# Softmax of a group in its own iteration, between pieces of the product with V; the last V in quarters

## Chip, cores and metric

The kernel runs on one core of a Trainium2 chip. The metric is the device time of one execution in microseconds; the median of three runs counts. The engines are TensorE (PE, its weight loads PEld), VectorE (DVE), ScalarE (ACT), GpSimd (POOL) and SyncE (SP), which here only issues transfers.

## What is computed

One decode step of a transformer block: layer norm, attention of one new token over a cache of 4,096 keys and values, then a second layer norm and a small MLP. Four batches, 32 heads, head size 128, all in bf16.

```python
B, Sq, D = 4, 1, 640;  H, Sk, Dh = 32, 4096, 128;  F = 1728
q = (layernorm(x) @ wq).reshape(B, Sq, H, Dh).transpose(0, 2, 1, 3)
scores = einsum("bhqd,bhkd->bhqk", q, k_cache) * Dh ** -0.5
o = einsum("bhqk,bhkd->bhqd", softmax(scores), v_cache)
h = x + o.transpose(0, 2, 1, 3).reshape(B, Sq, H * Dh) @ wo
y = layernorm(h) @ w1 + b1
h2 = h + (y * tanh(softplus(y))) @ w2
```

K and V are 134 MB each, and each element is used once. Everything else is small: wq and wo have 5.2 MB each, w1 and w2 together 4.4 MB.

## The kernel before

The 128 pairs of batch and head are taken in 32 groups of four heads of one batch: group g has head block `hq = g // 4` and batch `b = g % 4`. A group's K is one tile `kt` of 4.19 MB, its V one tile `vt` of the same size; 32 partitions belong to each head, and each partition holds 128 keys. There are two buffers for K and two for V.

**Scores.** `mul_and_sum` (L328) handles half of the keys (a part), in two steps: VectorE multiplies 64 of the 128 columns of `kt` by the query in place (L337), then TensorE adds the products up by eight matmuls with the identity (L344) into `s`, which has two buffers. After the second step `finish_sum` (L353) has VectorE add the last eight columns into `s_sb` (L356). So a group has four multiplies, four passes of eight matmuls, and two sums.

**Softmax.** `softmax` (L363) is a generator with two steps. First: VectorE takes the maximum of each partition (`pm`, L367) and TensorE transposes it (`tr`, L369). Second: VectorE takes the maximum of each head (`mx`, L374), TensorE spreads it over the partitions (L382), ScalarE copies it (`nbs`, L384) and makes four exponentials into `e2` (L387), which has two buffers.

**Product with V.** `pv_moving` (L241) makes 32 matmuls (L245) into `p`, which ScalarE copies to `p_sb` (L253, one buffer). `add_blocks` (L255) adds its four diagonal blocks into `ot` by small matmuls (L259). Groups 30 and 31 use `pv` (L267) after the loop instead: 128 small matmuls with V as the stationary operand (L271).

**The loop** (L397). The order of each engine's instructions is the order in which the program writes them. In iteration g, part 0 makes the scores of g, and between its two steps comes the second sum of g - 1 and the first step of its softmax; after the second step of part 0 comes the second step of that softmax. In part 1, between its two steps, come the first sum of g, `add_blocks(g - 2)`, and when b is 1 also `row_sums` (L283, L291) and `normalise` (L294) of the head block before. After part 1 SP issues the load of K for g + 2, which waits until the scores have read the buffer; then comes the product for g - 1; sometimes `project` (L318); then SP issues V of g + 1, which waits until the product has read its buffer. For the first seven iterations the queries of the next head block follow (L191, L205). The last K and the last V are loaded in two halves each (L93).

**After the loop** SP issues w1 (L463) and w2 (L464 to L467); w1 and most of w2 share one K buffer. Then come the second sum and the softmax of group 31, `pv(30)`, `row_sums`, `pv(31)`, `normalise`, `project`, the layer norm and the MLP. The first matrix product of the MLP (L514) writes `h1_ps`, part of which VectorE clears first (L509).

Of the kernel before, what the change touches and what calls it, by code (L numbers as in the profile page):

```python
# [8 lines left out]
FP32 = mybir.dt.float32  # L9
# [7 lines left out]
def kernel(  # L17
# [23 lines left out]
    nc = tc.nc  # L41

    B, Sq, D = A_x.shape
    _, H, Sk, Dh = A_k_cache.shape
    F = B_w1.shape[1]
    N = B * Sq
# [3 lines left out]
    R = Sk // PH  # L50
    NP = 2
# [3 lines left out]
    NG = HQ * N  # L55
# [14 lines left out]
    FREM = F - C2 * 128  # L70
    FC = C2 + 1
# [6 lines left out]
    kpool = ctx.enter_context(tc.tile_pool(name="kpool", bufs=KBUFS))  # L78
    vpool = ctx.enter_context(tc.tile_pool(name="vpool", bufs=VBUFS))
# [5 lines left out]
    out_rows = out.rearrange("b s (c p) -> (b s c) p", p=128)  # L85


    def load_kv(pool, tag, cache, g):
        hq, b = divmod(g, N)
        t = pool.tile([128, R, Dh], BF16, tag=tag, name=f"{tag}{g}")  # L90
        view = cache[b, G * hq : G * (hq + 1)].rearrange("h (p r) d -> (h p) r d", p=PH)

        np_ = NP if g == NG - 1 else 1  # L93
        for i in range(np_):
            r0, r1 = i * R // np_, (i + 1) * R // np_
            nc.sync.dma_start(out=t[:, r0:r1, :], in_=view[:, r0:r1, :])
        return t

    def load_k(g):
        return load_kv(kpool, "kt", A_k_cache, g)  # L100

    def load_v(g):
        return load_kv(vpool, "vt", A_v_cache, g)

    x_bf = consts.tile([N, D], BF16)
    nc.scalar.dma_start(out=x_bf[:, :], in_=x_rows[:, :])
# [63 lines left out]
    ps = ps_cm.__enter__()  # L170
# [58 lines left out]

    J = 4  # L230
    NSTAT = 2

    def ot_of(g):
        hq, b = divmod(g, N)
        if b == 0:
            ot[hq] = ps.tile([128, N, G], FP32, tag="ot", name=f"ot{hq}")
        return ot[hq][:, b, :]

    blocks = {}

    def pv_moving(g):  # L241
        vt = vts.pop(g)
        p_ps = ps.tile([J * G, J * Dh], FP32, tag="p", name=f"p{g}")
        for r in range(0, R, J):
            nc.tensor.matmul(  # L245
                p_ps[:, :],
                lhsT=e2[g % NE2][:, r : r + J, :].rearrange("p j q -> p (j q)"),
                rhs=vt[:, r : r + J, :].rearrange("p j d -> p (j d)"),
                start=(r == 0),
                stop=(r == R - J),  # L250
            )
        blocks[g] = work.tile([J * G, J * Dh], FP32, tag="p_sb", bufs=1, name=f"p_sb{g}")
        nc.scalar.copy(out=blocks[g][:, :], in_=p_ps[:, :])  # L253

    def add_blocks(g):  # L255
        o = ot_of(g)
# [10 lines left out]
    def pv(g):  # L267
        vt = vts.pop(g)
        o = ot_of(g)
        for r in range(R):  # L270
            nc.tensor.matmul(  # L271
                o,
                lhsT=vt[:, r, :],
                rhs=e2[g % NE2][:, r, :],
                start=(r == 0),
                stop=(r == R - 1),
            )
# [15 lines left out]
    def normalise(hq):  # L293
        nc.vector.tensor_tensor(  # L294
            out=otn[:, hq, :, :],
            in0=ot.pop(hq)[:, :, :],
            in1=rls.pop(hq)[:, :, :],
            op=ALU.mult,
        )
# [28 lines left out]
    def mul_and_sum(g, part):  # L328

        hq, b = divmod(g, N)  # L330
        r0 = part * RP
        kt = kts[g][:, r0 : r0 + RP, :]
        s_ps = ps.tile([128, RP, W], FP32, tag="s", bufs=2, name=f"s{g}_{part}")
        s_of[g, part] = s_ps
        for k in range(NQ):
            d0 = k * DQ
            nc.vector.tensor_tensor(  # L337
                out=kt[:, :, d0 : d0 + DQ],
                in0=kt[:, :, d0 : d0 + DQ],
                in1=qbs[:, hq, b, d0 : d0 + DQ].unsqueeze(1).to_broadcast([128, RP, DQ]),  # L340
                op=ALU.mult,
            )
            for d in range(d0, d0 + DQ, W):
                nc.tensor.matmul(  # L344
                    s_ps[:, :, :],
                    lhsT=ident[:, :],
                    rhs=kt[:, :, d : d + W],
                    start=(d == 0),
                    stop=(d == Dh - W),
                )  # L350
            yield

    def finish_sum(g, part):  # L353
        if part == 0:
            s_sbs[g] = work.tile([128, R], FP32, tag="s_sb", name=f"s_sb{g}")
        nc.vector.tensor_reduce(  # L356
            out=s_sbs[g][:, part * RP : (part + 1) * RP],
            in_=s_of.pop((g, part))[:, :, :],
            axis=AX.X,
            op=ALU.add,  # L360
        )

    def softmax(g):  # L363

        s_sb = s_sbs.pop(g)
        pm = work.tile([128, 1], FP32, tag="pm", name=f"pm{g}")
        nc.vector.tensor_reduce(out=pm[:, :], in_=s_sb[:, :], axis=AX.X, op=ALU.max)  # L367
        tr_ps = ps.tile([128, 128 + G], FP32, tag="tr", name=f"tr{g}")
        nc.tensor.matmul(  # L369
            tr_ps[0:1, 0:128], lhsT=pm[:, :], rhs=ident_f[:, :], start=True, stop=True  # L370
        )
        yield
        mx = work.tile([1, G], FP32, tag="mx", name=f"mx{g}")
        nc.vector.tensor_reduce(  # L374
            out=mx[:, :],
            in_=tr_ps[0:1, 0:128].rearrange("o (a b) -> o a b", a=G),
            axis=AX.X,
            op=ALU.max,
        )

        nb_ps = tr_ps[:, 128 : 128 + G]
        nc.tensor.matmul(nb_ps, lhsT=nscale[:, :], rhs=mx[:, :], start=True, stop=True)  # L382
        nb = work.tile([128, G], FP32, tag="nbs", name=f"nbs{g}")
        nc.scalar.copy(out=nb[:, :], in_=nb_ps)  # L384
        for q in range(G):
            p0, p1 = q * PH, (q + 1) * PH
            nc.scalar.activation(  # L387
                out=e2[g % NE2][p0:p1, :, q],
                in_=s_sb[p0:p1, :],
                func=ACT.Exp,  # L390
                bias=nb[p0:p1, q : q + 1],
                scale=SCALE,
                accum_out=rs2[p0:p1, g, q : q + 1],
            )
        yield

    for g in range(NG):  # L397
        hq, b = divmod(g, N)
        for part in range(NP):
            now = mul_and_sum(g, part)  # L400
            before = None
            next(now)
            if part > 0:
                finish_sum(g, part - 1)
                if 2 <= g < NG - NSTAT + 2:
                    add_blocks(g - 2)
                    if b == 1:
                        row_sums(hq - 1)
                        normalise(hq - 1)
            elif g >= 1:  # L410
                finish_sum(g - 1, NP - 1)
                before = softmax(g - 1)
                next(before)
            next(now)
            if before is not None:
                next(before)
        kts.pop(g)
        if g + 2 < NG:
            kts[g + 2] = load_k(g + 2)
        if 1 <= g < NG - NSTAT + 1:  # L420
            pv_moving(g - 1)
        if g in PROJ_AT:
            project(PROJ_AT[g])
        if g + 1 < NG:
            vts[g + 1] = load_v(g + 1)
        for n in Q_AT.get(g, ()):
            q_chunk(n)
            q_broadcast(n)
        if g in WO_AT:

            if not wo_sb:
                wo_sb.append(wbig.tile([128, H, D], BF16, tag="w", name="wo_sb"))
            h0 = WO_AT[g] * WOC
            nc.sync.dma_start(
                out=wo_sb[0][:, h0 : h0 + WOC, :],
                in_=A_wo.rearrange("(h p) n -> p h n", p=128)[:, h0 : h0 + WOC, :],
            )
            if WO_AT[g] == 0:
                nc.sync.dma_start(out=b1_row[:, :], in_=B_b1.rearrange("(o f) -> o f", o=1))
        if g == B1_AT:  # L440
            b_ps = ps.tile([128, FC], FP32, tag="small", name="b_ps")
            for c in range(FC):
                cols, fw = f_chunk(b1_row[:, :], c)
                nc.tensor.matmul(
                    b_ps[0:fw, c : c + 1],
                    lhsT=cols,
                    rhs=ident[0:1, 0:1],
                    start=True,
                    stop=True,
                )  # L450
            nc.vector.tensor_copy(out=b1T[:, 0:C2], in_=b_ps[:, 0:C2])
            nc.vector.tensor_copy(out=b1T[0:FREM, C2:FC], in_=b_ps[0:FREM, C2:FC])
# [13 lines left out]
    for k in range(CK):  # L466
        nc.sync.dma_start(out=w2_sb[:, k], in_=w2_view[:, k])  # L467


    finish_sum(NG - 1, NP - 1)  # L470
    for _ in softmax(NG - 1):
        pass
    pv(NG - 2)
    row_sums(HQ - 1)
    pv(NG - 1)
# [29 lines left out]
    nc.vector.tensor_tensor(out=sq[:, :, :], in0=hc[:, :, :], in1=hc[:, :, :], op=ALU.mult)  # L505


    h1_ps = ps.tile([128, FC, N], FP32, tag="qq", name="h1_ps")
    nc.vector.memset(h1_ps[FREM:128, FC - 1, :], 0.0)  # L509
    rstd = mlp.tile([128, N], FP32)  # L510
    for c in range(FC):
        fw = f_chunk(w1_sb[:, 0, :], c)[1]
# [119 lines left out]
```

## Time and profile before

| | us |
|---|---|
| median of three runs (671.48 to 672.41) | 671.55 |
| the profiled execution | 672.24 |
| its span, first to last instruction | 670.4 |
| PE busy (3,121 matmuls) | 562.8 |
| DVE busy | 351.6 |
| ACT busy | 112.2 |
| transfers of the large queue, share of 16 engines' span | 98.6% |
| HBM read | 283.35 MB |

Times are measured from the start of the span. In the lines quoted below, a group reads: line, engine, operation, tile written <- tiles read, shape, count, busy time, mean ns of one, idle time before it and what ended it. A line of the timeline reads: start, duration, engine, line, operation, tiles, count, and in brackets the idle time of the engine before it with what released it. The mean granted clock of TensorE is 0.94 of full speed.

### The profile page before, as it was taken

The page shows a single profiled execution, that of the slowest core. Times are in us where ns is not written, and L with a number is a line of the kernel's source. Part 1 is how long each engine was busy: PE and PEld are TensorE (multiplying, and loading weights), DVE is VectorE, ACT ScalarE, POOL GpSimd, SP SyncE. Part 2 cuts the span into 40 slices and gives each one's busy share as a digit, 9 for nine tenths or more (in the row PEclk, how much of TensorE's full clock was granted, in tenths as well). Part 3 has the DMA queues.
Part 4 walks back from the last instruction along what each step waited for, and adds up shares of the span by engine and source line. Part 5 has one row for each costly group of instructions (what it writes and reads, how often), then busy time and mean ns, then how long its engine had stood idle before and what let it go on. Part 6 is the DMA issues. An engine that isn't in the chain of part 4 may idle for free.

```text
span 670.4 us, 7163 instructions
## 1 busy us (share of the span) xinstructions
PE 562.8 (84%) x3121; PEld 255.9 (38%) x3121; DVE 351.6 (52%) x304; ACT 112.2 (17%) x343; POOL 2.4 (0%) x13
## 2 busy tenths in 40 slices
PE   0589999799998886688998899869987899888985
PEld 0234444344443342233443344333433344333454
DVE  2385455455654456336664444666543566644642
ACT  0021121221220111011110111111101111110131
POOL 1000000000000000000000000000000000000000
PEclk9999999899997997878999899898999799997995
DMA  9999999999999999999999999999999999999994
GB/s 374 438 437 436 427 429 427 437 436 435 429 428 427 428 425 428 430 428 430 431 437 436 431 431 425 436 434 435 431 434 425 436 435 432 435 429 428 434 414 175
DMA packets 15191, 283.81 MB, mean 423 GB/s; under 512 B 1267, under 2 KB 5559, under 8 KB 6584
## 3 DMA queue, kind: packets, MB, share of 16 engines
q1 hardware_dynamic: 15152, 283.36, 98.6%
q8 instruction: 24, 0.39, 0.2%
q14 instruction: 7, 0.06, 0.0%
q10 hardware_dynamic: 8, 0.01, 0.0%
HBM read 283.35 MB, written 0.01 MB: 423 GB/s over the span
## 4 chain that ended last, share of the span: by engine, by line
PE 45%; DMA 34%; DVE 19%; issue 1%; ACT 1%; SPq 0%; DVEq 0%
DMA kt<-in_A_k_cache_dram 34%; PE s L344 21%; DVE kt L337 16%; PE p L245 15%; PE ot L259 3%; PE q_ps L191 1%; PE qb_ps L205 1%; PE ot L271 1%; PE tr L369 1%; DVE mx L374 1%; DVE s_sb L356 1%; ACT q_all L198 1%; PE l_ps L283 0%; PE h_ps L514 0%; PE yT L318 0%
## 5 line engine op out<-in xcount | busy, mean ns | idle before, releaser
L337 DVE TENSOR_TENSOR kt<-kt,qbs 128x4096 bf16<-128x4096 bf16 x128 | 291.4, 2279 | 211.6 <-DMA kt<-in_A_k_cache_dram 211.6
L344 PE MATMUL s<-kt,ident 128*128 128x512 bf16 x1024 | 262.9, 404 | 77.1 <-DVE kt L337 77.0
L245 PE MATMUL p<-vt,e 128*16 128x512 bf16 x960 | 215.8, 384 | 0.0
L344 PEld LDWEIGHTS <-ident 128*128 128x128 bf16 x1024 | 99.2, 102 | 197.5 <-issue 97.2
L245 PEld LDWEIGHTS <-e 128*16 128x16 bf16 x960 | 84.7, 91 | 131.0 <-issue 20.2
L387 ACT ACTIVATE e<-s_sb,nbs 32x128 bf16<-32x128 f32 x128 | 73.9, 577 | 2.5
L253 ACT COPY p_sb<-p 16x512 f32<-16x512 f32 x30 | 17.2, 574 | 317.9 <-PE p L245 317.9
L356 DVE TENSOR_REDUCE s_sb<-s 128x64 f32<-128x512 f32 x64 | 43.4, 679 | 3.8 <-PE s L344 3.7
L374 DVE TENSOR_REDUCE mx<-tr 1x4 f32<-1x128 f32 x32 | 8.9, 277 | 50.0 <-PE tr L369 49.8
L384 ACT COPY nbs<-tr 128x4 f32<-128x4 f32 x32 | 5.2, 162 | 173.0 <-PE tr L382 173.0
L259 PEld LDWEIGHTS ot<-ident_f,p_sb 16*128 16x128 f32 x240 | 28.9, 186 | 12.7 <-issue 12.7
L387 ACT ACTIVATION_READ_ACCUMULATOR e<-s_sb,nbs 32x1 f32 x128 | 32.1, 251 | 0.0
L259 PE MATMUL ot<-ident_f,p_sb 16*128 16x4 f32 x240 | 31.5, 250 | 0.0
L191 PE MATMUL q_ps<-wq_sb,xT 128*4 128x512 bf16 x40 | 11.0, 409 | 9.8 <-DMA wq_sb<-in_A_wq_dram 9.8
L382 PEld LDWEIGHTS tr<-mx,nscale 1*128 1x128 f32 x64 | 9.4, 183 | 13.8 <-issue 13.1
L291 DVE RECIPROCAL rl<-l_ps 128x16 f32<-128x16 f32 x8 | 2.1, 257 | 23.0 <-PE l_ps L283 23.0
L369 PE MATMUL tr<-ident_f,pm 128*1 128x128 f32 x64 | 12.9, 285 | 1.2 <-DVE pm L367 1.2
L205 PE MATMUL qb_ps<-q_all,sel 4*128 4x128 bf16 x128 | 9.2, 225 | 5.3 <-ACT q_all L198 5.3
L382 PE MATMUL tr<-mx,nscale 1*128 1x4 f32 x64 | 12.2, 258 | 0.4 <-DVE mx L374 0.4
L205 PEld LDWEIGHTS <-sel 4*128 4x128 bf16 x128 | 8.4, 98 | 9.1 <-issue 9.1
L198 ACT CAST q_all<-q_ps 4x512 bf16<-4x512 f32 x8 | 4.6, 574 | 35.4 <-PE q_ps L191 35.4
L367 DVE TENSOR_REDUCE pm<-s_sb 128x1 f32<-128x128 f32 x32 | 9.2, 286 | 1.1
(79 smaller groups left out, 75.1 us busy)
## 6 DMA issues: line engine op xcount, KB each, us to landing
kt<-in_A_k_cache_dram SPq DMA_DIRECT2D x31, 4096.0 KB, 23.8
vt<-in_A_v_cache_dram SPq DMA_DIRECT2D x31, 4096.0 KB, 26.5
wq_sb<-in_A_wq_dram SPq DMA_DIRECT2D x1, 5120.0 KB, 15.4
wo_sb<-in_A_wo_dram SPq DMA_DIRECT2D x4, 1280.0 KB, 29.0
kt<-in_A_k_cache_dram SPq DMA_DIRECT2D x2, 2048.0 KB, 19.0
vt<-in_A_v_cache_dram SPq DMA_DIRECT2D x2, 2048.0 KB
w<-in_B_w_dram SPq DMA_DIRECT2D x1, 2160.0 KB, 21.2
w<-in_B_w_dram SPq DMA_DIRECT2D x3, 640.0 KB, 19.5
```

Source lines behind the costliest of these rows:

```text
L191: nc.tensor.matmul(q_ps[:, :], lhsT=xT[:, c, :], rhs=wq_sb[:, c, n * QC : (n + 1) * QC], start=(c == 0), stop=(c == DC - 1),)
L205: nc.tensor.matmul(qb_ps[:, b * Dh : (b + 1) * Dh], lhsT=sel[:, b, q, :], rhs=q_all[:, h * Dh : (h + 1) * Dh], start=(q == 0), stop=(q == ...
L245: nc.tensor.matmul(p_ps[:, :], lhsT=e2[g % NE2][:, r : r + J, :].rearrange("p j q -> p (j q)"), rhs=vt[:, r : r + J, :].rearrange("p j d - ...
L253: nc.scalar.copy(out=blocks[g][:, :], in_=p_ps[:, :])
L259: nc.tensor.matmul(o, lhsT=p_sb[:, j * Dh : (j + 1) * Dh], rhs=ident_f[0 : J * G, j * G : (j + 1) * G], start=(j == 0), stop=(j == J - 1),)
L337: nc.vector.tensor_tensor(out=kt[:, :, d0 : d0 + DQ], in0=kt[:, :, d0 : d0 + DQ], in1=qbs[:, hq, b, d0 : d0 + DQ].unsqueeze(1).to_broadcas ...
L344: nc.tensor.matmul(s_ps[:, :, :], lhsT=ident[:, :], rhs=kt[:, :, d : d + W], start=(d == 0), stop=(d == Dh - W),)
L356: nc.vector.tensor_reduce(out=s_sbs[g][:, part * RP : (part + 1) * RP], in_=s_of.pop((g, part))[:, :, :], axis=AX.X, op=ALU.add,)
L369: nc.tensor.matmul(tr_ps[0:1, 0:128], lhsT=pm[:, :], rhs=ident_f[:, :], start=True, stop=True)
L374: nc.vector.tensor_reduce(out=mx[:, :], in_=tr_ps[0:1, 0:128].rearrange("o (a b) -> o a b", a=G), axis=AX.X, op=ALU.max,)
L382: nc.tensor.matmul(nb_ps, lhsT=nscale[:, :], rhs=mx[:, :], start=True, stop=True)
L387: nc.scalar.activation(out=e2[g % NE2][p0:p1, :, q], in_=s_sb[p0:p1, :], func=ACT.Exp, bias=nb[p0:p1, q : q + 1], scale=SCALE, accum_out=r ...
```

## The change

Iteration g now makes the scores of g without anything of group g - 1's softmax between them. After them come the second sum of g and its softmax, whose two steps stand between pieces of the product of g - 1: eight matmuls, first step, eight matmuls, second step, sixteen matmuls. `add_blocks` and `row_sums` move from part 1 to part 0; `normalise` moves behind the first step of the softmax. The softmax of group 31 is therefore made at the end of its iteration, ahead of the issues of w1 and w2 in the program, and the clearing of `h1_ps` moves up before `pv(30)`. The last V is loaded in four quarters instead of two halves; the last K stays in halves.

```diff
--- before.py
+++ after.py
@@ -85,22 +85,22 @@
     out_rows = out.rearrange("b s (c p) -> (b s c) p", p=128)
 
 
-    def load_kv(pool, tag, cache, g):
+    def load_kv(pool, tag, cache, g, parts):
         hq, b = divmod(g, N)
         t = pool.tile([128, R, Dh], BF16, tag=tag, name=f"{tag}{g}")
         view = cache[b, G * hq : G * (hq + 1)].rearrange("h (p r) d -> (h p) r d", p=PH)
 
-        np_ = NP if g == NG - 1 else 1
+        np_ = parts if g == NG - 1 else 1
         for i in range(np_):
             r0, r1 = i * R // np_, (i + 1) * R // np_
             nc.sync.dma_start(out=t[:, r0:r1, :], in_=view[:, r0:r1, :])
         return t
 
     def load_k(g):
-        return load_kv(kpool, "kt", A_k_cache, g)
+        return load_kv(kpool, "kt", A_k_cache, g, NP)
 
     def load_v(g):
-        return load_kv(vpool, "vt", A_v_cache, g)
+        return load_kv(vpool, "vt", A_v_cache, g, 2 * NP)
 
     x_bf = consts.tile([N, D], BF16)
     nc.scalar.dma_start(out=x_bf[:, :], in_=x_rows[:, :])
@@ -229,6 +229,7 @@
 
     J = 4
     NSTAT = 2
+    PAUSES = (R // 4, R // 2)
 
     def ot_of(g):
         hq, b = divmod(g, N)
@@ -239,6 +240,7 @@
     blocks = {}
 
     def pv_moving(g):
+
         vt = vts.pop(g)
         p_ps = ps.tile([J * G, J * Dh], FP32, tag="p", name=f"p{g}")
         for r in range(0, R, J):
@@ -249,8 +251,11 @@
                 start=(r == 0),
                 stop=(r == R - J),
             )
+            if r + J in PAUSES:
+                yield
         blocks[g] = work.tile([J * G, J * Dh], FP32, tag="p_sb", bufs=1, name=f"p_sb{g}")
         nc.scalar.copy(out=blocks[g][:, :], in_=p_ps[:, :])
+        yield
 
     def add_blocks(g):
         o = ot_of(g)
@@ -397,28 +402,29 @@
     for g in range(NG):
         hq, b = divmod(g, N)
         for part in range(NP):
-            now = mul_and_sum(g, part)
-            before = None
-            next(now)
-            if part > 0:
-                finish_sum(g, part - 1)
-                if 2 <= g < NG - NSTAT + 2:
+            for k, _ in enumerate(mul_and_sum(g, part)):
+                if k > 0:
+                    continue
+                if part > 0:
+                    finish_sum(g, part - 1)
+                elif 2 <= g < NG - NSTAT + 2:
                     add_blocks(g - 2)
                     if b == 1:
                         row_sums(hq - 1)
-                        normalise(hq - 1)
-            elif g >= 1:
-                finish_sum(g - 1, NP - 1)
-                before = softmax(g - 1)
-                next(before)
-            next(now)
-            if before is not None:
-                next(before)
         kts.pop(g)
         if g + 2 < NG:
             kts[g + 2] = load_k(g + 2)
-        if 1 <= g < NG - NSTAT + 1:
-            pv_moving(g - 1)
+
+        now = pv_moving(g - 1) if 1 <= g < NG - NSTAT + 1 else iter(())
+        finish_sum(g, NP - 1)
+        steps = softmax(g)
+        next(now, None)
+        next(steps)
+        if b == 1 and hq > 0:
+            normalise(hq - 1)
+        next(now, None)
+        next(steps)
+        next(now, None)
         if g in PROJ_AT:
             project(PROJ_AT[g])
         if g + 1 < NG:
@@ -466,10 +472,10 @@
     for k in range(CK):
         nc.sync.dma_start(out=w2_sb[:, k], in_=w2_view[:, k])
 
-
-    finish_sum(NG - 1, NP - 1)
-    for _ in softmax(NG - 1):
-        pass
+    h1_ps = ps.tile([128, FC, N], FP32, tag="qq", name="h1_ps")
+    nc.vector.memset(h1_ps[FREM:128, FC - 1, :], 0.0)
+
+
     pv(NG - 2)
     row_sums(HQ - 1)
     pv(NG - 1)
@@ -505,8 +511,6 @@
     nc.vector.tensor_tensor(out=sq[:, :, :], in0=hc[:, :, :], in1=hc[:, :, :], op=ALU.mult)
 
 
-    h1_ps = ps.tile([128, FC, N], FP32, tag="qq", name="h1_ps")
-    nc.vector.memset(h1_ps[FREM:128, FC - 1, :], 0.0)
     rstd = mlp.tile([128, N], FP32)
     for c in range(FC):
         fw = f_chunk(w1_sb[:, 0, :], c)[1]
```

## The prediction

> **What bounds the kernel now.** I read the slices of the page first, then the waits of the big groups, then the order of time at three places.
>
> ```profile
> DMA  9999999999999999999999999999999999999994
> GB/s 374 438 437 436 427 429 427 437 436 435 429 428 427 428 425 428 430 428 430 431 437 436 431 431 425 436 434 435 431 434 425 436 435 432 435 429 428 434 414 175
> ...
> L337 DVE TENSOR_TENSOR kt<-kt,qbs 128x4096 bf16<-128x4096 bf16 x128 | 291.4, 2279 | 211.6 <-DMA kt<-in_A_k_cache_dram 211.6
> L344 PE MATMUL s<-kt,ident 128*128 128x512 bf16 x1024 | 262.9, 404 | 77.1 <-DVE kt L337 77.0
> ```
> The transfer engines are full in 39 of 40 slices; VectorE loses 211.6 us waiting for K, and TensorE waits for VectorE. So transfers set the pace: K lands about every 19.3 us (574.91, then 594.23). A compute change can pay only at the end, where the last slice falls to 175 GB/s, or cost if a load is issued too late. The page's chain names PE for 45% only because an issue waits for the product that frees a buffer; the transfers already queued hide that wait. In the stretch 150 to 200 us K took 19.8 to 22.9 us from issue to landing, while 4.19 MB at 434 GB/s need 9.7: at the tightest some 10.1 us of other transfers are still ahead. That is the margin before anything starves.
>
> An iteration that K does not hold up (group 30), by starts:
> ```profile
> 619.45 1.90 PE L344 MATMUL s<-kt,ident 128*128 128x512 bf16 x8
> 621.28 0.38 PE L369 MATMUL tr<-ident_f,pm 128*1 128x128 f32 x2
> 623.42 0.38 PE L382 MATMUL tr<-mx,nscale 1*128 1x4 f32 x2
> 624.22 1.89 PE L344 MATMUL s<-kt,ident 128*128 128x512 bf16 x8 [0.42 <-DVE kt L337]
> 626.04 1.05 PE L259 MATMUL ot<-ident_f,p_sb 16*128 16x4 f32 x8
> 628.86 7.07 PE L245 MATMUL p<-vt,e 128*16 128x512 bf16 x32
> ```
> TensorE runs almost without a hole: 9.4 us from the first score matmul to the product, 7.0 of product, 16.4 together. The end:
> ```profile
> 645.88 0.69 DVE L356 TENSOR_REDUCE s_sb<-s 128x64 f32<-128x512 f32 x1 [1.99 <-PE s L344]
> 648.10 3.40 PE L271 MATMUL ot<-e,vt 128*128 128x4 bf16 x128
> 651.79 1.90 PE L271 MATMUL ot<-e,vt 128*128 128x4 bf16 x66
> 655.21 1.79 PE L271 MATMUL ot<-e,vt 128*128 128x4 bf16 x62 [1.52 <-issue]
> 659.54 0.06 DVE L509 MEMSET h_ps<- 64x4 f32 x1
> 659.66 0.94 PE L514 MATMUL h_ps<-h2T,w 128*128 128x4 bf16 x25 [0.63 <-DVE h_ps L509]
> ```
> The last product stops for 1.52 us after 66 of its 128 matmuls. Its second half of V begins at matmul 65, so that half had landed: the hole is no wait for V, and the profile calls it issue.
>
> **The change, part by part.** *Softmax in its own iteration, in the middle.* Nothing is removed; L356, L367, L369, L374, L382 and the exponentials move. After the scores of g, VectorE does its second sum and maximum while TensorE does eight matmuls of the product (8 x 0.219 = 1.75 us, the step of L245). The tail of before shows this path alone: sum at 645.88, maximum at 646.60, transpose at 647.03, so 1.26 us after the scores end (645.77); 1.75 covers it. From transpose to the second small matmul it took 0.75 (647.03 to 647.78), again under 1.75. ScalarE needs 0.4 + 0.2 + 2.4 us and 16 matmuls take 3.5, so the block copy L253 waits little, and the first score pass covers it. The product section thus grows from 7.0 to 7.0 + 2 x 0.31 = 7.6.
>
> The score section loses those 0.62, but L259 moves to part 0. VectorE's first sum now waits for 1.83 + 0.98 + 1.83 = 4.64 us of TensorE; then 0.1 to start, 0.6 for the sum and 2.3 for the fourth multiply put the last pass at 7.7, while TensorE has reached only 6.5. The section is 7.7 + 1.8 = 9.5 (9.4 before), the iteration 17.1 against 16.4: 0.7 longer where TensorE sets it. Behind the sum and maximum on VectorE stand the multiplies of the next group; they begin about 2.5 us after the scores, their first result is there at 4.9, and TensorE asks at 7.6: covered.
>
> Where K sets it (group 28: K at 574.91, K issue at 587.50): before 12.5 us to the end of scores. After, the sum and maximum no longer stand between the first multiplies, so the fourth starts at 7.7 and scores end at 11.9; with 7.6 of product 19.5, as before (12.5 + 7.0).
>
> *Do loads come late?* V waits for the product and K for the scores, both on SP, in the same order as before. In groups 1 to 6, with the query chunk, the K issues of before stand 19.21 apart (151.89, 171.10); after about 19.9, and six such add some 4.3 us. Of the 10.1 us about 6 are left, and the later groups at 17.1 regain 2 each against 19.3. Cost: nothing. Without this cover it would be paid one for one.
>
> *Groups 29 to 31, where TensorE runs ahead of nothing any more.* In group 29 TensorE waits on L291 and its multiply: 2.75 us idle at 605.28, then passes of 3.57 instead of 1.9.
> ```profile
> 605.31 0.26 DVE L291 RECIPROCAL rl<-l_ps 128x16 f32<-128x16 f32 x1 [2.68 <-PE l_ps L283]
> 608.03 3.57 PE L344 MATMUL s<-kt,ident 128*128 128x512 bf16 x8 [2.75 <-DVE kt L337]
> ```
> The granted clock is 0.50 from 607 to 613 us. Idle of 2.33 (before 235.43) left it at 1.00, 2.58 (before 308.99) did not. After, L291 sits in part 0 and the hole is some 2.65, as L294 no longer follows it: by the nearest row it is slow again. The slow stretch then lies over passes that VectorE's sum holds up anyway, scores end about 16.6 us after K (594.23) instead of 17.3, and the product of 28 ends near 618.4 rather than 619.5. Then 17.1 + 0.5 (L318) + 9.5: scores of 31 end at 645.5, against 645.77. If the clock holds, 644.2. I take -0.2, ends -1.6 and, if also the 2.2 us hole at 594.4 slows it, +2.
>
> The Trainium skill (TensorE: Matmul & The Clock Gate, Part 1) has the clock drop only after a free-running window of about 3.4 us idle. The rows above differ, with 2.58 and 2.75; by the rule this term would be -1.6, by the rows -0.2.
>
> *Last V in quarters.* Two more issues on SP, 0.33 to 0.43 each, move L463 from 637.24 to about 638. From 636 us on 10.2 MB were still moved, 8.6 of them issued later, so 1.6 MB (3.8 us) cover this. In the built order the last two pieces of w2 also wait for the first two quarters; the first half landed near 647.8 (SP's last wait began then), and w1 fills the queue until 658.4. Cost nothing. The gain is nothing too if the hole of 1.52 stays, 1.5 if smaller transfers shorten it.
>
> The Trainium skill (Runtime: NRT & Kernel Launch, Instruction fetch mechanics) says that instructions come in blocks of 256 and that crossing one is mostly hidden. The holes at 653.69 and 661.58 lie some 256 TensorE instructions apart, and the page shows 24 instruction packets for 0.39 MB; so I read both as late instruction blocks, which the rule would price near nothing and the row at 1.52. I let the row stand.
>
> *L509 earlier.* h2T is written at 659.06; as otn at 657.04 let L318 start at 657.27, L514 could start at 659.3 instead of 659.66: -0.37. If the hole of 0.34 before 661.92 is fixed in time, 0.
>
> *A floor.* The first matmul of L514 needs w1, issued at 637.24 and landed 21.2 later, at 658.44. Whatever the front of the tail gains, L514 cannot start before about 658.6: all gains together stop at 1.1 us.
>
> Sum: -0.2 (groups 29 to 31) + 0 (quarters) - 0.37 (memset) = -0.6, with ends 0 and -1.1 where nothing is late; I take -0.5, as the second hole may eat part. The profiled execution took 672.24, its span 670.4, 0.69 above the median of 671.55; span 669.9, median 671.05.
>
> **Rivals.** *The stream ends sooner.* Between the K landings at 496.16 and 516.89 lie 20.73 us instead of 19.3, with TensorE and the queue both fed. If other issue times avoid this, 1.4 goes with the 0.5: 669.65. For it: the loss is in the transfers, so the floor moves along. Against: no step of this change touches its cause that I can see, and slices range from 425 to 438 without a pattern.
>
> *The pieces are not covered (slower).* Place: the two small matmuls inside the product. The bare path takes 2.3 us (645.77 to 648.10), 1.7 above the 0.6 counted. If the eights do not hide it, each early iteration costs 0.7 + 1.7 = 2.4 more, six cost 14.5, 10.1 are hidden, and the transfers stand still for 4.4 us: 676.0. It decides from about 1.7 per iteration in all (10.1 / 6), and in the tail from 2 us at the end of the scores of 31 (with the hole kept, 673.2). Against: VectorE has nothing else to do at that point.
>
> *The change does nothing at all:* if both holes keep their place in time, 671.55. It lies in the forecast's range.
>
> **How the numbers follow.** About 0.2% (1.34 us) is what a measurement of this kernel tells from no change. Forecast, tail gain 0 to 1.1 or a slip under 1.3: 0.56, its own range 670.2 to 672.5. Stream sooner, with a quicker tail: 0.19. Pieces not covered, or the tail slipping past 1.34: 0.25. Predicted 671.05; the range 669.6 to 673.6 takes in the first rival and the tail slip of the second. Faster 0.19, same 0.56, slower 0.25.
>
> **What would show it.** Right: K landings still near 19.3 us apart and no slice under 425 GB/s that was above it; L245 split in time by L369 and L382 with no hole over 0.5 us; scores of 31 ending at 644 to 646; L514 starting between 658.6 and 659.5. Wrong: transfers idle before 640 us, the hole in the last product gone and the span over 1.3 us shorter (then something other than w1 set the end), or VectorE late for the first score pass of a group.

## The result, and the profile after

| | before | after |
|---|---|---|
| median of six runs each, us | 671.71 | 676.14 |
| span of the profiled execution, us | 670.4 | 675.4 |
| waits of the four multiplies for K, us in total | 211.6 | 68.4 |

The ratio is 1.0064, 95% interval 1.0053 to 1.0076: 4.4 us slower. The forecast was 671.05, and at most 673.6. The two profiled executions took 672.24 and 677.16, the second the slowest of its six, so the profiles show a difference of about 5.0.

Line numbers of the changed kernel are up to five higher: L337 is now L342, L344 is L349, L356 is L361. In the brackets of the profile, "issue" is idle time in which the engine waited for nothing that the profile shows. The page of the changed kernel first: the transfers by slices (a slice is 16.9 us), and the groups by cost.

```profile
DMA  9999999989999999999999999999999999999994
GB/s 371 435 434 435 434 435 435 432 355 422 408 430 435 420 418 422 433 439 434 429 426 426 435 434 435 434 435 432 434 433 432 435 432 433 428 433 427 433 414 167
...
L349 PE MATMUL s<-kt,ident 128*128 128x512 bf16 x1024 | 258.2, 404 | 83.5 <-DVE kt L342 83.4
L342 DVE TENSOR_TENSOR kt<-kt,qbs 128x4096 bf16<-128x4096 bf16 x128 | 287.0, 2277 | 68.4 <-DMA kt<-in_A_k_cache_dram 68.4
...
L361 DVE TENSOR_REDUCE s_sb<-s 128x64 f32<-128x512 f32 x64 | 44.3, 691 | 154.5 <-PE s L349 154.5
```

and the sums in the kernel before:

```profile
L356 DVE TENSOR_REDUCE s_sb<-s 128x64 f32<-128x512 f32 x64 | 43.4, 679 | 3.8 <-PE s L344 3.7
```

Two things stand out. The ninth slice (135 to 152 us) has 355 GB/s where before had 436: for the first time the transfer engines run short of work in mid-kernel. And VectorE's waits changed sides: 143 us less for K, while the sums (L361) now wait 154.5 us for TensorE. That is no loss by itself: between 70 and 200 us TensorE waits for no K in either kernel, so it sets the time of the K issues there, 19.21 us apart before and 20.00 after (iterations with queries and without row sums). A K and a V together take about 19.3 us to transfer (8.39 MB at 434 GB/s). So before, the transfers ahead of a K kept their length: the K issued at 70.65 took 23.4 us to land, the one at 109.06 took 24.0. After, each iteration uses some of them up: 15.8 us for the K issued at 97.70, 15.4 at 117.70, 12.2 at 141.88. Looked at in stretches of two microseconds (the columns: stretch, its length, busy time of PE, PEld, DVE, ACT and POOL with counts, granted clock, share and rate of the transfers), the hole is sharp:

```profile
138.00:140.00 2.00, 0.68 (x4) 0.23 (x3) 1.91 (x1) 0.00 (x0) 0.00 (x0) 1.00 1.18 508
140.00:142.00 2.00, 2.00 (x9) 0.74 (x9) 0.11 (x1) 0.00 (x0) 0.00 (x0) 1.00 0.23 98
142.00:144.00 2.00, 2.00 (x12) 0.94 (x11) 1.02 (x4) 0.00 (x0) 0.00 (x0) 1.00 0.90 262
144.00:146.00 2.00, 2.00 (x11) 0.88 (x10) 2.00 (x2) 0.03 (x1) 0.00 (x0) 1.00 0.64 279
```

The second of these stretches in the kernel before, and then the K issue of the same iteration, first after and then before:

```profile
140.00:142.00 2.00, 1.34 (x15) 0.79 (x14) 0.00 (x0) 0.85 (x2) 0.00 (x0) 1.00 0.99 426
...
141.88 0.33 SPq L96 DMA_DIRECT2D kt<-in_A_k_cache_dram  x1
...
132.69 0.33 SPq L96 DMA_DIRECT2D kt<-in_A_k_cache_dram  x1
```

SyncE issued a K at 141.88 in this kernel and at 132.69 before. This issue ends the longest of the early iterations, the first with row sums: 24.2 us, and 23.6 before. Two more holes of the same kind follow the K issues at 161.88 and 181.88: 303 GB/s over 162 to 166 us and 328 over 182 to 186, where before had 426 and 442. Over 140 to 146 it is 213 against 431. The missing bytes amount to 3.0 + 1.2 + 1.0 = 5.2 us of transfer time, by (431 - 213) / 431 x 6 and so on. K of group 24 then lands at 500.81 instead of 496.16, 4.65 later.

Where was the time before 141.88 lost? In the timeline of the changed kernel, iteration 0:

```profile
41.85 1.24 PE L191 MATMUL q_ps<-wq_sb,xT 128*4 128x512 bf16 x5
...
42.20 1.28 ACT L392 ACT_TABLE_LOAD   x1
...
45.61 0.25 ACT L392 ACTIVATION_READ_ACCUMULATOR e<-s_sb,nbs 32x1 f32 x1
45.88 0.57 ACT L198 CAST q_all<-q_ps 4x512 bf16<-4x512 f32 x1
...
46.51 1.05 PE L205 MATMUL qb_ps<-q_all,sel 4*128 4x128 bf16 x16 [3.41 <-ACT q_all L198]
...
57.70 0.33 SPq L96 DMA_DIRECT2D kt<-in_A_k_cache_dram  x1
```

and the same instructions in the kernel before:

```profile
39.06 1.24 PE L191 MATMUL q_ps<-wq_sb,xT 128*4 128x512 bf16 x5
...
40.34 0.57 ACT L198 CAST q_all<-q_ps 4x512 bf16<-4x512 f32 x1 [18.69 <-PE q_ps L191]
...
46.58 1.28 ACT L387 ACT_TABLE_LOAD   x1
...
51.44 0.33 SPq L96 DMA_DIRECT2D kt<-in_A_k_cache_dram  x1
```

The softmax of group 0 now stands ahead of the queries of head block 1, on TensorE as on ScalarE. TensorE first makes the two small matmuls of the softmax and waits 1.20 and 0.37 us for VectorE's maxima, with no product between; it starts the queries (L191) at 41.85 instead of 39.06. On ScalarE a table load and four exponentials stand in front of the copy of the queries; TensorE waits for that copy, which takes another 2.8 us, and behind it stand all scores of group 1. They start at 47.49 instead of 41.95, 5.5 us late, about half by each of the two, and the next K is issued 6.3 us late. After that the lag grows by 0.8 in each iteration (K issues at 77.70, 97.70 and 117.70 against 70.65, 89.85 and 109.06), to 9.2 at 141.88.

The end of the changed kernel, from the landing of K of group 29:

```profile
597.57 2.29 DVE L342 TENSOR_TENSOR kt<-kt,qbs 128x4096 bf16<-128x4096 bf16 x1 [4.89 <-DMA kt<-in_A_k_cache_dram]
...
599.91 2.92 PE L349 MATMUL s<-kt,ident 128*128 128x512 bf16 x8 [1.97 <-DVE kt L342]
...
607.66 5.18 PE L349 MATMUL s<-kt,ident 128*128 128x512 bf16 x16 [2.49 <-DVE kt L342]
...
623.61 1.90 PE L349 MATMUL s<-kt,ident 128*128 128x512 bf16 x8
...
649.08 1.89 PE L349 MATMUL s<-kt,ident 128*128 128x512 bf16 x8 [1.32 <-DVE kt L342]
...
656.97 1.93 PE L276 MATMUL ot<-e,vt 128*128 128x4 bf16 x67
...
660.25 1.77 PE L276 MATMUL ot<-e,vt 128*128 128x4 bf16 x61 [1.36 <-issue]
...
664.30 0.95 PE L518 MATMUL h_ps<-h2T,w 128*128 128x4 bf16 x25 [0.27 <-DVE h2T L504]
```

Group 30 starts its scores 26.0 us after that K (25.2 before), group 31 follows after 17.7 (16.9 before), and the scores of 31 end at 651.0 against 645.8. So in these two profiles 3.3 us come from the transfers and 1.9 from the last three groups; the tail behind is 0.2 shorter, and the span is 5.0 longer.

### The profile page after: what moved, and what is told of

It reads as the page before. It is cut to its first block, busy times and chain, and to the rows that moved or that the text cites. A ratio compares the mean times of both kernels' runs of the same rounds, so it can differ in the third digit from the quotient of the medians.

```text
span 675.4 us, 7162 instructions
## 1 busy us (share of the span) xinstructions
PE 557.2 (83%) x3121; PEld 259.6 (38%) x3121; DVE 355.6 (53%) x304; ACT 112.2 (17%) x343; POOL 2.4 (0%) x13
## 4 chain that ended last, share of the span: by engine, by line
PE 60%; DMA 19%; DVE 17%; ACT 1%; issue 1%; DVEq 0%; SPq 0%; ACTq 0%
PE s L349 26%; PE p L247 23%; DMA kt<-in_A_k_cache_dram 19%; DVE kt L342 13%; PE ot L264 4%; DVE s_sb L361 3%; PE tr L387 1%; PE qb_ps L205 1%; PE ot L276 1%; PE q_ps L191 1%; PE tr L374 1%; PE yT L323 1%; ACT q_all L198 1%; PE l_ps L288 0%; PE h_ps L518 0%
## 5 line engine op out<-in xcount | busy, mean ns | idle before, releaser
L349 PE MATMUL s<-kt,ident 128*128 128x512 bf16 x1024 | 258.2, 404 | 83.5 <-DVE kt L342 83.4
L342 DVE TENSOR_TENSOR kt<-kt,qbs 128x4096 bf16<-128x4096 bf16 x128 | 287.0, 2277 | 68.4 <-DMA kt<-in_A_k_cache_dram 68.4
L247 PE MATMUL p<-vt,e 128*16 128x512 bf16 x960 | 222.1, 379 | 0.0
L349 PEld LDWEIGHTS <-ident 128*128 128x128 bf16 x1024 | 101.8, 103 | 219.1 <-issue 117.4
L361 DVE TENSOR_REDUCE s_sb<-s 128x64 f32<-128x512 f32 x64 | 44.3, 691 | 154.5 <-PE s L349 154.5
L247 PEld LDWEIGHTS <-e 128*16 128x16 bf16 x960 | 81.5, 90 | 112.6 <-issue 12.7
L264 PEld LDWEIGHTS ot<-ident_f,p_sb 16*128 16x128 f32 x240 | 30.5, 195 | 13.8 <-issue 13.8
L264 PE MATMUL ot<-ident_f,p_sb 16*128 16x4 f32 x240 | 33.1, 257 | 0.0
L257 ACT COPY p_sb<-p 16x512 f32<-16x512 f32 x30 | 17.2, 574 | 29.7 <-PE p L247 29.7
L191 PE MATMUL q_ps<-wq_sb,xT 128*4 128x512 bf16 x40 | 11.0, 410 | 9.9 <-DMA wq_sb<-in_A_wq_dram 9.9
L374 PE MATMUL tr<-ident_f,pm 128*1 128x128 f32 x64 | 12.2, 272 | 2.4 <-DVE pm L372 2.4
L387 PE MATMUL tr<-mx,nscale 1*128 1x4 f32 x64 | 12.2, 258 | 0.7 <-DVE mx L379 0.7
L374 PEld LDWEIGHTS tr<-ident_f,pm 128*1 128x1 f32 x64 | 5.3, 84 | 11.0 <-issue 3.3
## 6 DMA issues: line engine op xcount, KB each, us to landing
w<-in_B_w_dram SPq DMA_DIRECT2D x1, 2160.0 KB, 19.6
w<-in_B_w_dram SPq DMA_DIRECT2D x3, 640.0 KB, 16.1
```

Source lines behind the costliest of these rows:

```text
L191: nc.tensor.matmul(q_ps[:, :], lhsT=xT[:, c, :], rhs=wq_sb[:, c, n * QC : (n + 1) * QC], start=(c == 0), stop=(c == DC - 1),)
L247: nc.tensor.matmul(p_ps[:, :], lhsT=e2[g % NE2][:, r : r + J, :].rearrange("p j q -> p (j q)"), rhs=vt[:, r : r + J, :].rearrange("p j d - ...
L264: nc.tensor.matmul(o, lhsT=p_sb[:, j * Dh : (j + 1) * Dh], rhs=ident_f[0 : J * G, j * G : (j + 1) * G], start=(j == 0), stop=(j == J - 1),)
L342: nc.vector.tensor_tensor(out=kt[:, :, d0 : d0 + DQ], in0=kt[:, :, d0 : d0 + DQ], in1=qbs[:, hq, b, d0 : d0 + DQ].unsqueeze(1).to_broadcas ...
L349: nc.tensor.matmul(s_ps[:, :, :], lhsT=ident[:, :], rhs=kt[:, :, d : d + W], start=(d == 0), stop=(d == Dh - W),)
L361: nc.vector.tensor_reduce(out=s_sbs[g][:, part * RP : (part + 1) * RP], in_=s_of.pop((g, part))[:, :, :], axis=AX.X, op=ALU.add,)
```

## The experiments

The theory was that two delays together dry the transfers up: the late start (5.5 us) and the longer iterations (0.8 each). With the changed kernel, which has both, e1, e2 and e3 make the square of the two, and e4 adds the late start to the kernel before. The times of e1 to e4 are compared with the kernel before, run on the same chip in the same job (672.02); the changed kernel was measured in another job, 4.4 us above the kernel before there.

**Late start undone (e1).** The queries of block 1 become the pieces between the softmax steps of iteration 0:

```diff
+    def queries(n):
+        q_chunk(n)
+        yield
+        q_broadcast(n)
+        yield
...
+        if g == 0:
+            now = queries(1)
...
-        for n in Q_AT.get(g, ()):
+        for n in Q_AT.get(g, ()) if g else ():
```

> Undoes one thing of the changed kernel: in iteration 0 the query chunk and its broadcast stand between the two steps of the softmax of group 0 instead of behind them. Theory (loads come late: group 0's softmax holds the query copy up on ScalarE, 5.5 us, and 0.8 us per iteration eat the rest of the margin until the transfers dry up near 141, 162 and 182 us): the K issue of iteration 1 falls from 57.7 to about 53, no 2-us window before 200 us is under 290 GB/s, K of group 29 lands near 593 to 594.5 instead of 597.6, time 671.5 to 673.5 (what the last three groups cost more stays). Rival (the longer iterations at the end and a slower transfer rate, not the start): time stays within 1 us of 676.1.

Median 672.47, ratio to before 1.0005 (0.9993 to 1.0017). The K issue of iteration 1 is at 52.36, the one that came at 141.88 is at 136.92, the rate over 140 to 146 us is 431 GB/s, and K of 29 lands at 594.16 (594.23 before). Some stretches of 2 us before 70 us are at 279 GB/s, below the 290 expected, but over the 6 us around each the rate is 434 or more. The extra cost of the last three groups did not stay, against the expectation: from K of 29 to the end of the scores of 31 it took 51.2 us, 53.4 in the changed kernel. So part of what e1 regains lies there, and the transfers' share is the 3.4 us by which K of 29 lands earlier. The late start is necessary for the loss; the longer iterations alone cost nothing that shows.

**Longer iterations undone (e2).** The block sums and row sums go back to part 1:

```diff
-                elif 2 <= g < NG - NSTAT + 2:
+                if part > 0 and 2 <= g < NG - NSTAT + 2:
                     add_blocks(g - 2)
```

> Undoes another thing alone: the block sums and row sums go back into part 1, behind the first sum. Theory: VectorE's fourth multiply no longer leaves TensorE idle for 1.3 us, an iteration that TensorE sets takes 16.2 to 16.4 us instead of 17.2; the late start (K issue of iteration 1 at 57 us) stays, but the lag no longer grows and the transfers never dry up; time 669.5 to 672. Rival (the late start alone dries the transfers up): a window under 290 GB/s before 200 us and a time of 674 or more.

Median 670.50, ratio 0.9977 (0.9967 to 0.9988): faster than the kernel before. The late start stays (K issue at 58.45), but the distance of the next ones is 18.9 us (77.36, 96.28, 115.19) instead of 20.0, the critical one comes at 138.24, and the rate over 140 to 146 us is 421; no stretch of 2 us between 4 and 200 us is under 290. In group 30 of this kernel,

```profile
619.05 5.35 PE L349 MATMUL s<-kt,ident 128*128 128x512 bf16 x24
...
624.34 1.05 PE L264 MATMUL ot<-ident_f,p_sb 16*128 16x4 f32 x8
...
625.73 1.89 PE L349 MATMUL s<-kt,ident 128*128 128x512 bf16 x8 [0.34 <-DVE kt L342]
...
627.55 1.89 PE L247 MATMUL p<-vt,e 128*16 128x512 bf16 x8
```

three passes run on end, the block sums fill the time in which VectorE sums and multiplies, and the hole before the fourth pass shrinks from 1.32 to 0.34 us: 8.5 us of scores, 16.1 with the product (16.2 to 16.4 were expected), against 17.2 in the changed kernel and 16.4 before. The scores of group 31 end at 644.3 instead of 645.8.

**Both undone (e3).** The two edits together.

> Both of the edits of the two runs before it, on the changed kernel. Theory: no window under 290 GB/s before 200 us, scores of the last group end at 645 or earlier, time 669 to 671.5, not slower than the kernel before. Rival (the rest of the change costs): above 673.

Median 670.49, ratio 0.9981 (0.9971 to 0.9991), no different from the run before it. The scores of group 31 end at 643.8, and no stretch of 2 us between 4 and 200 us is under 290 GB/s. With the transfers fed, an earlier start buys nothing.

**The late start alone, in the kernel before (e4).**

```diff
-            elif g >= 1:
+            elif g >= 2:
                 finish_sum(g - 1, NP - 1)
...
+        if g == 0:
+            finish_sum(0, NP - 1)
+            for _ in softmax(0):
+                pass
```

> The kernel before with one part of the change alone: the softmax of group 0 in its own iteration, ahead of the query chunk. Theory (the late start needs the longer iterations to bite): the K issue of iteration 1 moves from 51.4 to 56 or 57, K from issue to landing falls by 5 to 6 us in the first eight groups and stays over 13, the transfers don't dry up, time within 0.7 us of the kernel before. Rival (the late start alone is the cause): 674 or more.

Median 672.05, ratio 1.0009 (0.9995 to 1.0023). The start is as late as in the changed kernel (K issue at 56.71) and the critical issue at 138.26. K from issue to landing fell to 14.5 us (issue at 157.50), still over the 13 expected, though for the critical issue the profile gives no landing; the rate over 140 to 146 us is 399, a dent that costs nothing measurable. So neither delay alone is paid; together, in the changed kernel, they are. A lag of 5.6 us at the critical issue is still hidden, 9.2 is not.

**The tail edits alone, in the kernel before (e5).** Quarters of the last V and the early clearing of h1_ps.

```diff
-        np_ = NP if g == NG - 1 else 1
+        np_ = (2 * NP if tag == "vt" else NP) if g == NG - 1 else 1
...
+    h1_ps = ps.tile([128, FC, N], FP32, tag="qq", name="h1_ps")
+    nc.vector.memset(h1_ps[FREM:128, FC - 1, :], 0.0)
     pv(NG - 2)
```

> The kernel before with the two edits of the tail alone: last V in four quarters, the clearing of h1_ps ahead of the last products. Theory (the hole in the last product is a late block of instructions and stays; the clearing gives 0.37; the first product of the MLP can't start before w1 lands near 658.4): 0.2 to 0.8 us under the kernel before. Rival (the quarters shorten the wait for the last V): the hole goes and 1 us or more is gained.

Median 671.50 against 672.06, ratio 0.9990 (0.9981 to 0.9999), 0.6 us. The hole in the last product stays (1.26 us after 66 matmuls); the first product of the MLP follows its input by 0.27 instead of waiting for the clearing.

**The tail edits taken out of e3 (e6).** As e3, but V in halves and the clearing late.

> The kernel of e3 (queries of block 1 as pieces of iteration 0, block sums in part 1) with the last V in halves again and the clearing back in its late place. Theory: scores of the last group end at 643.8 as in e3, the first product of the MLP starts at 658.2 to 659 because w1 or the clearing holds it, within 0.6 us of e3 (670.5). Rival (e3's gain comes from the tail edits): 671.5 or more, like the kernel before.

Median 670.36, ratio 0.9975 (0.9965 to 0.9985), where e3 had 0.9981 in another job. The tail edits give nothing here. The lines of its end tell why:

```profile
649.55 1.85 PE L276 MATMUL ot<-e,vt 128*128 128x4 bf16 x64
...
652.75 2.11 PE L276 MATMUL ot<-e,vt 128*128 128x4 bf16 x64 [1.35 <-DMA vt<-in_A_v_cache_dram]
...
658.17 0.97 PE L526 MATMUL h_ps<-h2T,w 128*128 128x4 bf16 x25 [1.30 <-DMA w<-in_B_w_dram]
```

The first product waits 1.30 us for w1 whatever the last V does. With halves, the last product here does wait for V, after exactly 64 matmuls; with quarters it stops at the hole of the next experiment instead, for about as long.

**What the hole is (e7).** 32 more small matmuls in iteration 20, result unused.

> The kernel of e3 with 32 more small matmuls in iteration 20, whose result is not used. They move every later TensorE instruction 64 places on. Theory (the hole in the last product is a late block of 256 instructions): it moves from behind matmul 67 to about matmul 35 of the last product. Rival (it is a wait for V or another transfer): it stays behind matmul 64 to 67, or goes. Time within 0.7 us of e3 in both.

The last product in the timeline of this kernel:

```profile
649.68 1.07 PE L276 MATMUL ot<-e,vt 128*128 128x4 bf16 x35
...
652.16 2.62 PE L276 MATMUL ot<-e,vt 128*128 128x4 bf16 x93 [1.41 <-issue]
```

The hole moved from behind matmul 67 to behind matmul 35, by exactly the 32 pairs of weight load and matmul added (time of the one run 670.55). It belongs to a place in the instruction stream, not to a transfer of data. That fits the Trainium skill (Runtime: NRT & Kernel Launch, Instruction fetch mechanics), by which instructions arrive in blocks of 256. The same section calls the crossing of a block mostly hidden; here, if it is one, it shows for 1.4 us. TensorE goes through 256 instructions in 3.4 us just ahead of this place (the 128 pairs from 645.96), and the transfers move 400 GB/s or more over 648 to 654 us. Whether these two are the reason, or that a block came late at all, no run shows directly.

**Past w1 (e8 and e9).** w1 in two column parts, on the kernel of e3.

> The kernel of e3 with w1 loaded in two column parts (1024 and 704 of 1728), so that the first matmuls of the MLP need only the first. Theory (w1's landing is the floor of the tail): the first product starts about 1 us earlier, at 657 to 657.5, and the time falls by 0.5 to 1.3 us against e3, to 669.2 to 670, until the last w2 piece holds the second product. Rival (shorter pieces of rows make the transfers slower): no gain or up to 1 us lost.

Median 670.75, ratio 0.9982 (0.9974 to 0.9991): no gain. The first matmul of the MLP started at 656.58, but already the second waited 1.79 us for a transfer of w: the parts interleave in the buffer. So this run did not test its question. The next lays them apart (the rest of its edit leads the matmuls to the two parts):

```diff
+    w1_a = w12[:, 0 : DC * FA].rearrange("p (c f) -> p c f", c=DC)
+    w1_b = w12[:, DC * FA : DC * F].rearrange("p (c f) -> p c f", c=DC)
...
```

> As e8, but the two parts of w1 lie apart in the buffer, so that in the built order the matmul 41 of the first product of the MLP is the first to wait for the second part (in e8 it was matmul 2, so e8 did not test what it was made for). Theory (w1's landing is the floor of the tail in e3): the first product starts at 656.5 to 657.5 and the time falls to 669.2 to 670. Rival (another limit lies right behind): no gain against e3 (670.5).

Median 669.65 against 671.89, ratio 0.9973 (0.9964 to 0.9982); 0.8 us below e3, though in another job. The first product starts at 657.44 and follows its input, where in e3 it started at 658.20 after 1.34 us of waiting for w1. So w1 was the floor:

```profile
657.44 0.97 PE L539 MATMUL h_ps<-h2T,w 128*128 128x4 bf16 x25 [0.27 <-DVE h2T L525]
```

This is the fastest version of all, 2.2 us under the kernel before. The split itself was not timed beside e3 in one job, so its own share is less certain than the sum.

## Why the prediction was wrong

**The step that failed** is "Do loads come late?", with its "Cost: nothing". It set a lag of "some 4.3 us" against a margin of 10.1. Both numbers were off: the lag was 9.2 at the tightest issue, the margin some 7, and K of group 29 landed 3.3 us late. The prediction's own sign of being wrong, "transfers idle before 640 us", is what came.

- *The lag.* The 0.7 per iteration was right (0.8). Missing is the head: the softmax of group 0 moves too, and it has no product around it and the queries behind it. The prediction followed VectorE, TensorE and ScalarE only through an iteration with a product, and SyncE; it did not write out iteration 0. There TensorE waits for the maxima before it can start the queries (2.8 us), and the copy of the queries (L198) stands behind a table load of 1.28 us and four exponentials on ScalarE (2.8 more). That is 5.5 of the 9.2 us. e1 takes it away and the loss of the transfers goes with it.
- *The margin.* 10.1 came from issue to landing, less the time of one transfer. The transfers fell off from about 140 us on, 7.3 after the K issue of before (132.69), and e2 and e4 bound the hidden lag from below at 5.6. At 141.88, where the transfers had already run short, K still took 12.2 us to land, 2.5 more than the transfer of one K: so this measure shows 2.5 us ahead where nothing is, and it is too generous by about that. A lag of 4.3 would have been hidden by a margin of 7 too, so the missing head decides. One reading is that a landing waits for the slowest of the 16 engines while others are already out of work; in the tail of before their mean busy share falls step by step, 1.03, 0.72, 0.59 and 0.45 from 658 to 662 us. No run tests this.
- *What paces.* "So transfers set the pace" was read from waits added up over the whole run. It does not hold for the early groups, where TensorE waits for no K and already sets the issues in the kernel before; the 45% that the chain gives to PE are in part this, and not only issues that wait.

**The parts of the change were mostly sized right.** The product section with two pauses, 7.6 predicted, is 7.63 (615.97 to 623.60); the score section 9.5 is 9.57; the iteration 17.1 is 17.2, with queries 19.9 is 20.0. The pieces are covered: TensorE waits at neither small matmul, but for groups 0 and 31, which have no product around them. VectorE is in time for the first pass except where K itself is late. So the slower rival, "the pieces are not covered", named the right place of payment (loads late in the early groups, 676.0 against 676.1 measured), but its mechanism did not happen, and its number agrees by accident.

**Groups 29 to 31**, term -0.2 with an end of +2: from K of 29 to the end of the scores of 31 it took 53.4 us, 51.3 were forecast and 51.5 measured before. The named end came true: the clock dropped after the first hole already (1.97 us), so the first pass took 2.92 and the block sums behind it 1.86 instead of 1.05. In e1, which has the same order of instructions there, the hole was 1.42 us, the clock held through the first pass, and the stretch took 51.2, as forecast.

**Tail.** Quarters 0: right as far as it goes; where halves are late (e6) the hole takes their place. Clearing -0.37: right, the product follows h2T by 0.23 us (664.07 to 664.30) where it was 0.60. Floor by w1: right, but not reached in the changed kernel, where w1 landed 19.6 after its issue at 643.22, at 662.8, and L518 started at 664.30; e3 and e6 stop at it (658.2), and e9 passes it.

**The rival of a shorter stream** came half true and did not matter: the 20.73 us between two K landings at 496 to 517 are 19.3 in the changed kernel (500.81 to 520.13), which brings its delay from 4.65 to 3.3. In e1 and e3 the long distance is at the same place as before, in e4 it is at 418.81 to 439.66 instead. Its cause stays open.

## What to carry to other kernels

Moving a step one iteration forward moves it past something else at the very first iteration, where the work that was to hide it does not exist yet: write out iteration 0 on every queue, ScalarE's too. A margin of queued transfers is spent by the sum of all delays up to the tightest issue, so a late start that is free alone and a longer loop that is free alone can be paid together. And when two engines alternate, put independent work of the one where it waits for the other: an iteration that TensorE sets takes 17.2 us with the block sums in part 0 and 16.1 with them in part 1. Compare the length of an iteration with the time of its own transfers, stretch by stretch: 19.2 us against 19.3 kept the queue filled, 20.0 wore it down.

## What was unexpected of the hardware

The length of a hole did not decide whether TensorE's clock fell: 2.33 us left it at full speed in the kernel before, 1.97 us did not in the changed one, where the granted clock went from 1.00 to 0.50 between 600 and 601 us, while TensorE was already busy again, and stayed there until 610.6. Even the same hole went both ways: 2.11 us ahead of the first pass of group 29 left the clock at 1.00 in the kernel before, and in e5 it was 0.50 from 598 to 601. A decision in windows that run free of the program, as the Trainium skill has it (TensorE: Matmul & The Clock Gate, Part 1), fits that; its 3.4 us of idle were not needed here. No run shows such windows themselves.

TensorE stopped for 1.0 to 1.5 us inside the last product in the kernel before and in each profile with quarters, waiting for nothing that the profile shows, at a place that moved with the instruction count in e7.
